# Batch 0's queries cut as 192 and 256 instead of 256 and 192, with other loads at the start, in a fused attention and FFN kernel

## The chip, the core and the metric

The kernel runs on one core of a Trainium2 chip. Its time is the device time of one execution in microseconds; the median of several runs counts. A profile is one further execution, recorded by the hardware profiler. PE is TensorE, ACT is ScalarE, DVE is VectorE, POOL is GpSimd, SP is SyncE. Times within a profile are microseconds from the start of the span.

## The reference

Eight batches of attention with twelve heads, 448 tokens and head size 64, with a sigmoid in the place of the softmax, then a gated feed-forward network (FFN) over all 3584 tokens.

```python
scores = (1 / sqrt(64)) * q @ k.transpose(0, 1, 3, 2) - log(448)
attn = 1 / (1 + exp(-scores))
x = (attn @ v)                     # heads joined: 3584 x 768
gate = maximum(x @ w_gate, 0)      # 768 x 1536
val = x @ w_val                    # 768 x 1536
out = (gate * val) @ w_out         # 1536 x 768
```

Inputs and output are fp32 in memory; the kernel computes in fp16 with sums in fp32.

## The kernel before

**Tiles.** A batch's q, k and v lie in SBUF as fp16, 128 partitions by head pairs and token chunks. Twelve heads make three groups (g) of four heads, 448 tokens make seven chunks (c) of 64. `pe_transposes` (L201, copied out by DVE at L206) or, from batch 2 on, `dma_transposes` turn a group's k and q into `qkT`. `qk` (L232) computes scores for one chunk of keys in four 64x64 corners of the PE array, ACT takes the sigmoid into `PT` (L187), `pv` (L250) multiplies with v, and DVE scales the result into `xT` (L184). `gv` (L309) is one FFN unit: 128 of the 1536 hidden columns (f from 0 to 11), six matmuls for the gate and six for the value, then a relu (DVE at L320 or ACT at L318) and a product on DVE (L327) into `hT`.

**Order.** The program order is written by hand; each engine works through its own queue in that order. DMA issues stand in the queue of their engine as well: SP and ACT issue through hardware queues, POOL through a software queue, which also turns fp32 into fp16 on the way. POOL holds at most eight software loads in flight, since each waits for the semaphore of the eighth before it.

**Batch 0.** It is the stage that the change touches. Its queries are cut in two at `QCUT` = 4 chunks: `HALVES` are 256 queries and then 192. A `FirstSlot` is one group with one half: slots 0 to 2 are groups 0 to 2 with the first half, slots 3 to 5 the same with the second. A slot has four units `(i, u)`: three with two chunks of keys, one with a single chunk. A unit's scores go into one of two PSUM buffers (`pairp`), and one ACT instruction takes the sigmoid of all of it. The dictionary `after` says what PE does behind each unit: transposes of the next group, `keep_warm` (matmuls on zeros), `pv` of an earlier slot, or `ffn_mix(n)`, which takes n units from `gv_queue`. The queue is filled by `push_first(half, fs)`; a unit of half 0 needs the x of slots 0 to 2, one of half 1 that of slots 3 to 5. Four PSUM banks serve all the rest of this stage.

**Loads of batch 0.** The first four k chunks and the first `QCUT` q chunks of group 0 come in fp32 by SP and ACT into `ysb` tiles (L126) and are cast by DVE (L604) and ACT (L605). All else comes by POOL: the last three k chunks of group 0, k and the first q chunks of groups 1 and 2, the rest of group 0's q, v in three parts, then the FFN weights of two or three f at a time (`load_gv`, L148) between the loads of batch 1.

**Batch 1.** Its scores run in six bursts; behind each burst the tuple `mix` gives the count of `gv` units, and `hooks` place transposes among them: `(left, job)` runs the job when `left` units of that mix remain. From batch 2 on, the FFN uses sums of blocks to save products (L385); this part is not touched.

Of the kernel before, what the change touches and what calls it, by code (L numbers as in the profile page):

```python
# [17 lines left out]
def kernel(  # L18
# [10 lines left out]
    nc = tc.nc  # L29

    B, H, S, D = q.shape
# [4 lines left out]
    NCH = S // 64  # L36
    NDC = DM // P
    NFC = DF // P
    TW = 2 * NCH
    QCUT = 4  # L40
    HALVES = ((0, QCUT), (QCUT, NCH))

    qk_scale = 1.0 / math.sqrt(D)
# [59 lines left out]
    def rows_of(src, b):  # L103
        return src[b].rearrange("(x r) (t c) d -> (r t) x (c d)", r=2, c=NCH)

    def load(b, g0, g1, which, c0=0, c1=NCH):
        for nm, t16, src in zip("kq", tiles_of(b), (k, q)):
            if nm in which:
                xs, cs = slice(2 * g0, 2 * g1), slice(c0 * D, c1 * D)
                nc.gpsimd.dma_start(t16[:, xs, cs], rows_of(src, b)[:, xs, cs])  # L110

    def load_v(b):
        v16 = tiles_of(b)[2]
        nc.gpsimd.dma_start(v16[:, 0::2, :], rows_of(v, b)[:, 0::2, :])
        for r in range(2):
            nc.gpsimd.dma_start(
                v16[64 - 64 * r : P - 64 * r, 1::2, :], rows_of(v, b)[64 * r : 64 * r + 64, 1::2, :]
            )


    KCUT = 4
    first32 = []
    for src, c1, eng in ((k, KCUT, nc.sync), (q, QCUT, nc.scalar)):
        ysb = ysbp.tile([P, DM], FP32, tag="ysb", name="ysb")
        t32 = ysb[:, 0 : 2 * c1 * D].rearrange("p (x y) -> p x y", x=2)
        eng.dma_start(t32, rows_of(src, 0)[:, 0:2, 0 : c1 * D])  # L126
        first32.append(t32)
    zeros = early.tile([P, S], FP16, name="zeros")
    nc.vector.memset(zeros[:], 0.0)  # L129
    ident = early.tile([P, P], FP16, name="ident")  # L130
    make_identity(nc, ident[:])
    load(0, 0, 1, "k", KCUT)
    gate = const.tile([P, 2], FP16, name="gate")
    for g in range(1, NG):
        load(0, g, g + 1, "k")
        load(0, g, g + 1, "q", 0, QCUT)
    load(0, 0, 1, "q", QCUT)
    load_v(0)

    wg = wpool.tile([P, NDC, DF], FP16, name="wg")  # L140
    wv = wpool.tile([P, NDC, DF], FP16, name="wv")
# [2 lines left out]
    def load_gv(f0, f1, which=(0, 1)):  # L144
        fs = slice(f0 * P, f1 * P)
        for i in which:
            wt, src = ((wg, moe_w_gate), (wv, moe_w_val))[i]
            nc.gpsimd.dma_start(wt[:, :, fs], src[:, fs].rearrange("(c p) f -> p c f", p=P))  # L148
# [2 lines left out]
    load(0, 1, NG, "q", QCUT)  # L151
    load_gv(0, 2, (1,))
    load_gv(2, 4)
    load_gv(4, 6)
    load(1, 0, 1, "kq")
    load_gv(6, 9)
    load(1, 1, 2, "kq")
    load_v(1)
    load_gv(9, 12)
    load(1, 2, 3, "kq")  # L160

    def load_o():
        for m0, m1 in ((0, 512), (512, DM)):
# [31 lines left out]
    def pe_transposes(b, g, ti, c0=0, c1=NCH):  # L195
        t16 = in_tiles[b][ti]
        qkT = qkT_of(b, g)
        trt = bank16("trt")
        for c in range(c0, c1):
            for h in range(2):  # L200
                nc.tensor.transpose(  # L201
                    trt[64 * h : 64 * h + 64, c * P : (c + 1) * P],
                    t16[:, 2 * g + h, c * D : (c + 1) * D],
                    ident[:],
                )
        nc.vector.tensor_copy(  # L206
            qkT[:, ti * NCH + c0 : ti * NCH + c1, :].rearrange("p c x -> p (c x)"),
            trt[:, c0 * P : c1 * P],
        )
# [378 lines left out]
    def push_first(half, fs, act_relu=True):  # L588
        c0, c1 = HALVES[half]
        push_gv(0, 64 * c0, 64 * (c1 - c0), fs, act_relu)  # L590
# [12 lines left out]
    k16, q16, _ = in_tiles[0]  # L603
    nc.vector.tensor_copy(k16[:, 0:2, 0 : KCUT * D], first32[0])  # L604
    nc.scalar.copy(q16[:, 0:2, 0 : QCUT * D], first32[1])  # L605
    pe_transposes(0, 0, 0, 0, KCUT)
    pe_transposes(0, 0, 1, 0, QCUT)
    keep_warm(2)
    slots = [FirstSlot(half * NG + g, g, half) for half in range(2) for g in range(NG)]
    push_first(0, range(0, 6), False)  # L610
    def second_queries():
        for g in range(1, NG):
            pe_transposes(0, g, 1, QCUT, NCH)

    def pv_then_ffn(i):
        slots[i].pv()
        ffn_mix(1)

    def ffn_then_pv(i):
        ffn_mix(1)  # L620
        slots[i].pv()


    after = {
        (0, 0): lambda: pe_transposes(0, 0, 0, KCUT, NCH),
# [5 lines left out]
        (1, 2): lambda: pe_transposes(0, 2, 1, 0, QCUT),  # L631
        (1, 3): lambda: keep_warm(2),
        (2, 0): lambda: keep_warm(2),
        (2, 1): lambda: pe_transposes(0, 0, 1, QCUT, NCH),
        (2, 2): slots[0].pv,
        (2, 3): slots[1].pv,
        (3, 1): slots[2].pv,
        (3, 2): second_queries,
        (3, 3): lambda: ffn_mix(1),
        (4, 1): lambda: ffn_then_pv(3),  # L640
        (4, 3): lambda: ffn_mix(2),
        (5, 1): lambda: pv_then_ffn(4),
        (5, 3): lambda: ffn_mix(1),
    }
    for i, slot in enumerate(slots):
# [2 lines left out]
            if (i, u) in after:  # L648
                after[(i, u)]()
    slots[5].pv()  # L650
    push_first(1, range(0, 6))
    for f0 in range(6, 12, 2):
        for half in range(2):
            push_first(half, range(f0, f0 + 2))

# [59 lines left out]
    for b in range(1, B):  # L715
        if b == 1:
            cuts, pv_at = (0, 3, 6, 9, 13, 17, 21), {3: (0, 2), 5: (1, 2)}
        else:
            cuts, pv_at = (0, 4, 7, 11, 14, 18, 21), {0: (-1, 2), 2: (0, 2), 4: (1, 2)}
        bursts = list(range(len(cuts) - 1))  # L720
        inner = None
        if b > 2:
            inner = 4 * (b % 2)
            bursts.remove(inner + 1)
        count = len(bursts)
        hooks = {}
        if b == 1:
            mix = (3, 3, 3, 3, 3, 2)
            hooks = {
                1: [(1, lambda: both(1, 1))],  # L730
                3: [(1, lambda: both(1, 2))],
                4: [(3, lambda: dma_transposes(2, 0))],
                5: [(2, lambda: dma_transposes(2, 1)), (0, late_loads)],
            }
        elif b == 2:
            mix = (2, 2, 1, 1, 1, 2)
            hooks = {
                2: [(0, prepare)],
                4: [(0, lambda: weight_sums(0))],
                5: [(1, lambda: weight_sums(1)), (0, lambda: weight_sums(2))],  # L740
            }
            open_late()
        elif b == 3:
            mix = (1, 1, 1, 0, 0)
        else:
            mix = (0,) * count

        def burst(n):
            for i, (g, c) in enumerate(order[cuts[n] : cuts[n + 1]]):
                if n in pv_at and i == pv_at[n][1]:  # L750
                    if n == 0:
                        pv_finish(b - 1)
                        if b == 2:
                            push_group(0)
                        elif b % 2 == 0:
                            push_group(b // 2 - 1)
                    else:
                        pv_group(b, pv_at[n][0])
                qk_unit(b, g, c)

        for m in range(count):
            jobs = []
            burst(bursts[m])
            if m == 0 and b > 2:
                jobs.append(lambda: dma_transposes(b, 2))
            if b == 2 and m == count - 1:
                jobs.append(lambda: (dma_transposes(3, 0), dma_transposes(3, 1)))
            elif b == 3 and m == count - 1:
                jobs.append(lambda: (dma_transposes(4, 0), dma_transposes(4, 1)))
            elif 0 <= m - count + 2 and 3 < b < B - 1:  # L770
                jobs.append(lambda: dma_transposes(b + 1, m - count + 2))
            if b == 1:
                if m == 0:
                    load(2, 0, 1, "kq")
                    load(2, 1, 2, "kq")
                    load(2, 2, 3, "kq")
                    load_v(2)
            elif m == 0 and b + 1 < B:
                if b == 3:
                    jobs.append(lambda: hold(3, 2))  # L780
                jobs.append(lambda: (load(b + 1, 0, 3, "kq"), load_v(b + 1)))
            if b % 2 and b > 2:
                if m == count - 1:
                    jobs.append(lambda: (batch_sums_t1(b // 2), batch_sums(b // 2, (0, 1))))
            elif b > 3 and m == 0:
                jobs.append(lambda: batch_sums(b // 2 - 1, (1, HD)))
            if b == 2 and m == count - 1:
                ffn_mix(mix[m], hooks[m])
                next_work(jobs + [lambda: weight_sums(3)], first_act=True)
            elif mix[m]:  # L790
                for job in jobs:
                    job()
                ffn_mix(mix[m], hooks.get(m, ()))
            else:
                next_work(jobs, amid=(lambda: burst(inner + 1)) if m == inner else None)
            if b == 3 and m in (1, 3):
                for f in range(*((0, 8, 2), (8, NFC, 2))[m // 2]):
                    gate_sums(f, f + 2)
# [35 lines left out]
```

## Time and profile before

| | |
|---|---|
| runs, median (lowest to highest) | 393.48 us (393.33 to 394.0), 3 runs |
| profiled execution | 393.23 us, span 391.5 us |
| granted PE clock | 1.00 |
| PE busy | 385.4 us, 98% of the span |
| ACT busy, DVE busy | 224.8 us, 278.7 us |
| first sigmoid of batch 0 | 6.95 us |
| first `gv` unit | 19.22 us |
| `pv` of slot 5 | 30.42 to 31.12 us |
| first scores of batch 2 | 62.01 us |

The timeline gives each engine's instructions with the time at which a run of equal ones starts, its length and the idle time ahead of it. The chain in order of time follows the work that ended last back from the end. Matmul times overlap, since they are pipelined: the distance from one start to the next is what an instruction holds PE.

Landings of some loads of before, by the DMA issues of narrow windows (issue time plus time to landing): first k on SP 4.1, first q on ACT 4.4, k tail of group 0 6.75, k of group 1 7.95, last part of v 14.34, wg of f = 0 and 1 16.35, wv of the same 19.32, the last load of batch 1 49.3.

### The profile page before, as it was taken

What the parts mean: (1) busy time and instruction counts of PE and PEld (TensorE: products, weight loads), DVE (VectorE), ACT (ScalarE), POOL (GpSimd) and SP (SyncE); (2) the same over time, 40 slices, a digit from 0 to 9 for tenths busy, and PEclk for the clock granted to TensorE, in tenths of its full rate; (3) what the DMA queues carried; (4) which work ended last, traced back from release to release, by engine and by line L of the source; (5) the groups of instructions that cost most, each with busy time, mean ns of one, the idle gap of its engine ahead of it and who ended that gap; (6) DMA issues with size and microseconds to landing.
All of it is one profiled execution on the core that took longest, in us unless ns stands there. A gap on an engine that the chain in (4) does not pass through costs nothing.

```text
span 391.5 us, 8755 instructions
## 1 busy us (share of the span) xinstructions
PE 385.4 (98%) x3494; PEld 215.3 (55%) x3494; DVE 278.7 (71%) x540; ACT 224.8 (57%) x476; POOL 49.5 (13%) x73
## 2 busy tenths in 40 slices
PE   8999999999999999999999999999999999999995
PEld 4678786445455545454555554545455555555553
DVE  2453444367378789999757789999767779987663
ACT  5946778784877755555547764545475434533122
POOL 8644310500030300003000300000000000000000
PEclk9999999999999999999999999999999999999999
DMA  9999999998799891226945694233013320000135
GB/s 153 198 200 205 204 200 138 155 202 144 176 166 201 161 218 27 47 49 78 174 97 130 126 228 67 39 43 62 3 41 82 82 80 2 0 3 0 40 88 156
DMA packets 68953, 43.69 MB, mean 112 GB/s; under 512 B 35888, under 2 KB 65584, under 8 KB 68912
## 3 DMA queue, kind: packets, MB, share of 16 engines
q0 software_dynamic: 30736, 23.33, 39.7%
q1 hardware_dynamic: 37664, 19.24, 23.9%
q10 hardware_dynamic: 512, 0.56, 0.5%
q8 instruction: 27, 0.44, 0.4%
q14 instruction: 14, 0.11, 0.1%
HBM read 47.19 MB, written 11.01 MB: 149 GB/s over the span
## 4 chain that ended last, share of the span: by engine, by line
PE 96%; ACT 2%; DVE 1%; issue 0%
PE u L385 33%; PE g L385 16%; PE qk_ps L232 9%; PE y L385 9%; PE pv_ps L250 8%; PE g_ps L309 8%; PE v_ps L309 7%; PE ya L346 3%; ACT PT L187 2%; PE yb L346 1%; PE trt L201 1%; PE warm_ps L175 1%; DVE qkT L206 0%; DVE ysb L483 0%; DVE zeros L129 0%
## 5 line engine op out<-in xcount | busy, mean ns | idle before, releaser
L187 ACT ACTIVATE PT<-qk_ps 128x448 f16<-128x448 f32 (+3 forms) x318 | 150.8, 587 | 77.8 <-PE qk_ps L232 77.7
L385 PEld LDWEIGHTS <-S 128*128 128x128 f16 x540 | 52.8, 98 | 43.6 <-issue 0.2
L554 DVE TENSOR_TENSOR gsb<-g,gsb 128x448 f32<-128x448 f32 x72 | 42.8, 624 | 13.6 <-PE g L385 13.3
L232 PE MATMUL qk_ps<-qkT 64*64 64x448 f16 (+2 forms) x756 | 47.3, 335 | 0.9 <-DVE qkT L206 0.5
L327 DVE TENSOR_TENSOR hT<-gate_sb,v_ps 128x256 f16<-128x256 f32 (+2 forms) x36 | 16.2, 465 | 34.0 <-ACT gate_sb L318 18.0
L550 ACT COPY gsb<-u 128x448 f32<-128x448 f32 x48 | 25.6, 558 | 24.0 <-PE u L385 22.9
L385 PEld LDWEIGHTS <-hT 128*128 128x128 f16 x294 | 27.5, 98 | 21.3 <-issue 4.7
L421 ACT ACTIVATE ysb<-u 128x384 f32<-128x384 f32 x28 | 13.7, 490 | 42.7 <-PE u L385 40.6
L184 DVE TENSOR_SCALAR xT<-pv_ps 128x448 f16<-128x448 f32 (+2 forms) x53 | 27.9, 567 | 13.3 <-PE pv_ps L250 12.0
L250 PE MATMUL pv_ps<-PT,v 64*64 64x448 f16 (+2 forms) x756 | 36.5, 329 | 0.0
L309 PE MATMUL g_ps<-xT,wg 128*128 128x256 f16 (+2 forms) x216 | 33.5, 291 | 0.1
L309 PE MATMUL v_ps<-xT,wv 128*128 128x256 f16 (+2 forms) x216 | 33.3, 290 | 0.0
L385 PEld LDWEIGHTS <-wg 128*128 128x128 f16 x216 | 20.1, 98 | 21.8 <-issue 4.3
L385 PEld LDWEIGHTS <-wv 128*128 128x128 f16 x216 | 21.1, 98 | 19.7
L232 PEld LDWEIGHTS <-qkT 64*64 64x64 f16 x756 | 17.8, 105 | 21.8 <-issue 13.5
L250 PEld LDWEIGHTS <-v 64*64 64x64 f16 x756 | 21.4, 107 | 11.1 <-issue 0.7
L439 DVE SCALAR_TENSOR_TENSOR ysb<-y,ysb 128x384 f32<-128x384 f32 x24 | 13.4, 557 | 18.2 <-PE y L385 10.4
L385 PE MATMUL u<-T,hT 128*128 128x384 f16 x138 | 26.2, 326 | 0.0
L309 PEld LDWEIGHTS <-wg 128*128 128x128 f16 x216 | 18.5, 98 | 11.7 <-issue 5.1
L110 POOL DMA_DIRECT2D k<-in_k_dram x14 | 10.9, 777 | 109.1 <-DVE rel L215 102.7
L309 PEld LDWEIGHTS <-wv 128*128 128x128 f16 x216 | 20.2, 98 | 7.4
L385 PE MATMUL u<-xT,wg 128*128 128x448 f16 x108 | 23.5, 354 | 0.0
(69 smaller groups left out, 532.2 us busy)
## 6 DMA issues: line engine op xcount, KB each, us to landing
out_dram<-ysb SPq DMA_DIRECT2D x52, 192.0 KB, 3.0
k<-in_k_dram POOLq DMA_DIRECT2D x5, 672.0 KB, 11.7
q<-in_q_dram POOLq DMA_DIRECT2D x5, 672.0 KB, 14.5
v<-in_v_dram POOLq DMA_DIRECT2D x8, 336.0 KB, 14.7
v<-in_v_dram POOLq DMA_DIRECT2D x16, 168.0 KB, 14.0
k<-in_k_dram POOLq DMA_DIRECT2D x8, 224.0 KB, 12.0
wo<-in_moe_w_out_dram POOLq DMA_DIRECT2D x1, 1536.0 KB, 11.2
q<-in_q_dram POOLq DMA_DIRECT2D x6, 224.0 KB, 12.3
```

The lines of the kernel that those rows point to most:

```text
L184: nc.vector.tensor_scalar(out=xT, in0=src, scalar1=XSCALE, scalar2=None, op0=AOP.mult)
L187: nc.scalar.activation(PT_ap, ps_ap, AF.Sigmoid, bias=sig_bias, scale=qk_scale)
L232: nc.tensor.matmul(out_of(hh)[o : o + 64, :], qkT[rows, c, cols], qkT[rows, NCH + c0 : NCH + c1, cols], start=True, stop=True, tile_positi ...
L250: nc.tensor.matmul(ps[hh][64 * r : 64 * r + 64, 0:qn], v16[rows, 2 * g + hh, c * D : (c + 1) * D], pieces[c][rows, hh, :], start=(c == 0), ...
L309: nc.tensor.matmul(ps[-1][:, 0:qn], wt[:, dc, f * P : (f + 1) * P], xT_tiles[b][:, dc, q0 : q0 + qn], start=(dc == 0), stop=(dc == NDC - 1),)
L327: nc.vector.tensor_tensor(out=hT_tiles[g][:, f, o : o + qn], in0=gate_sb[:, 0:qn], in1=ps[1][:, 0:qn], op=AOP.mult,)
L346: nc.tensor.matmul(ps[:, 0 : m1 - m0], hT_tiles[g][:, f, t * P : (t + 1) * P], wo[:, f, m0:m1], start=(f == 0), stop=(f == NFC - 1),)
L385: nc.tensor.matmul(ps[:, 0:n], A[:, k_, :], W[:, k_, :], start=(first and k_ == 0), stop=(k_ == kn - 1), skip_group_check=True,)
L421: nc.scalar.activation(o, ps[:, 0:HM], AF.Copy, scale=OUT_SCALE)
L439: nc.vector.scalar_tensor_tensor(out=o, in0=ps[:, 0:HM], scalar=OUT_SCALE, in1=o, op0=AOP.mult, op1=AOP.add)
L550: by(gs[u][i][:], ps[u][:, 0:S])
L554: nc.vector.tensor_tensor(out=gs[u][i][:], in0=ps[u][:, 0:S], in1=gs[u][i][:], op=AOP.add)
```

## The change

The first part of batch 0's queries becomes 192, the second 256. The last three k chunks of group 0 come in fp32 by SP, behind the first k load, and ACT casts them, ahead of the first sigmoid. POOL loads v before the rest of group 0's queries. Among the later loads, batch 1's k and q come between weights at other places, and the last `load_gv` is parted. The rest of group 0's q is transposed behind unit (2, 3) instead of (2, 1), where a `keep_warm` stands now; `pv` of slot 2 and the second queries' transposes come one unit earlier. In slots 3 to 5 four `gv` units of 192 columns run instead of six of 256; batch 1 has 19 units in its mixes instead of 17.

```diff
-    QCUT = 4
+    QCUT = 3
...
-    for src, c1, eng in ((k, KCUT, nc.sync), (q, QCUT, nc.scalar)):
+    for src, c0, c1, eng in (
+        (k, 0, KCUT, nc.sync), (q, 0, QCUT, nc.scalar), (k, KCUT, NCH, nc.sync)
+    ):
         ysb = ysbp.tile([P, DM], FP32, tag="ysb", name="ysb")
-        t32 = ysb[:, 0 : 2 * c1 * D].rearrange("p (x y) -> p x y", x=2)
-        eng.dma_start(t32, rows_of(src, 0)[:, 0:2, 0 : c1 * D])
+        t32 = ysb[:, 0 : 2 * (c1 - c0) * D].rearrange("p (x y) -> p x y", x=2)
+        eng.dma_start(t32, rows_of(src, 0)[:, 0:2, c0 * D : c1 * D])
...
-    load(0, 0, 1, "k", KCUT)
     gate = const.tile([P, 2], FP16, name="gate")
     for g in range(1, NG):
         load(0, g, g + 1, "k")
         load(0, g, g + 1, "q", 0, QCUT)
+    load_v(0)
     load(0, 0, 1, "q", QCUT)
-    load_v(0)
...
     load_gv(2, 4)
+    load(1, 0, 1, "kq")
     load_gv(4, 6)
-    load(1, 0, 1, "kq")
+    load(1, 1, 2, "kq")
     load_gv(6, 9)
-    load(1, 1, 2, "kq")
     load_v(1)
-    load_gv(9, 12)
+    load_gv(9, 12, (0,))
     load(1, 2, 3, "kq")
+    load_gv(9, 12, (1,))
...
     nc.scalar.copy(q16[:, 0:2, 0 : QCUT * D], first32[1])
+    nc.scalar.copy(k16[:, 0:2, KCUT * D : NCH * D], first32[2])
...
-    push_first(0, range(0, 6), False)
+    push_first(0, range(0, 4), False)
...
+    def first_queries():
+        pe_transposes(0, 0, 1, QCUT, NCH)
+        slots[1].pv()
...
-        (2, 1): lambda: pe_transposes(0, 0, 1, QCUT, NCH),
+        (2, 1): lambda: keep_warm(2),
         (2, 2): slots[0].pv,
-        (2, 3): slots[1].pv,
-        (3, 1): slots[2].pv,
-        (3, 2): second_queries,
+        (2, 3): first_queries,
+        (3, 0): slots[2].pv,
+        (3, 1): second_queries,
         (3, 3): lambda: ffn_mix(1),
-        (4, 1): lambda: ffn_then_pv(3),
-        (4, 3): lambda: ffn_mix(2),
-        (5, 1): lambda: pv_then_ffn(4),
+        (4, 1): lambda: pv_then_ffn(3),
+        (4, 3): lambda: ffn_mix(1),
+        (5, 1): slots[4].pv,
         (5, 3): lambda: ffn_mix(1),
...
-    push_first(1, range(0, 6))
-    for f0 in range(6, 12, 2):
+    push_first(1, range(0, 4))
+    for f0 in range(4, 12, 2):
...
-            mix = (3, 3, 3, 3, 3, 2)
+            mix = (3, 3, 3, 4, 4, 2)
```

## The prediction

> **What bounds the kernel now.** I began with the page's busy shares and its chain that ended last.
>
> ```profile
> PE 385.4 (98%) x3494; PEld 215.3 (55%) x3494; DVE 278.7 (71%) x540; ACT 224.8 (57%) x476; POOL 49.5 (13%) x73
> PE 96%; ACT 2%; DVE 1%; issue 0%
> ```
>
> TensorE sets the end, except for 2% of ScalarE. The busy times by stretch say where PE ever idles.
>
> ```profile
> 5.00:17.34 12.34, 11.45 (x232) 6.98 (x231) 4.57 (x11) 10.08 (x13) 10.03 (x14) 1.00 1.35 191
> 17.34:31.12 13.78, 13.78 (x273) 10.97 (x273) 8.12 (x22) 8.01 (x12) 5.96 (x9) 1.00 1.40 200
> ```
>
> Columns: stretch, length, busy time of PE, PEld, DVE, ACT and POOL, granted clock, DMA share, GB/s. PE idles 0.89 us before 17.34 and not at all in the 13.78 us after it; the later stretches show 0.06 us up to 62.01 and none from there to the last matmul at 387.5. So every microsecond of PE time lost or won in the first stage reaches the end of the program. The chain in order of time shows what holds PE before 17.34:
>
> ```profile
> 10.11 0.44 PE qk_ps L232 x8
> 10.55 0.02 issue
> 10.58 3.35 ACT PT L187 x4
> 13.92 0.02 issue
> 13.94 3.35 ACT PT L187 x4
> 17.30 0.04 issue
> 17.34 0.36 PE qk_ps L232 x8
> ```
>
> A slot here is one group of four heads times one part of the queries: four units of scores, then their sigmoids. Slots 1 and 2 (256 queries) are bound by ScalarE, 3.36 and 3.40 us from start to start. PE fills that time with score matmuls, transposes and keep_warm, because no FFN work exists until x is complete for three groups. The timeline of ScalarE shows the other regime:
>
> ```profile
> 17.34 2.60 ACT L187 ACTIVATE PT<-qk_ps 128x768 f16<-128x768 f32 x4
> 21.11 1.51 ACT L187 ACTIVATE PT<-qk_ps 128x768 f16<-128x768 f32 x2 [1.16 <-PE qk_ps L232]
> 23.55 1.19 ACT L187 ACTIVATE PT<-qk_ps 128x768 f16<-128x768 f32 x2 [0.94 <-PE qk_ps L232]
> 26.65 1.51 ACT L187 ACTIVATE PT<-qk_ps 128x768 f16<-128x768 f32 x2 [1.91 <-PE qk_ps L232]
> 29.10 1.19 ACT L187 ACTIVATE PT<-qk_ps 128x768 f16<-128x768 f32 x2 [0.94 <-PE qk_ps L232]
> ```
>
> A slot of 192 queries costs ScalarE 2.62 us, and in slots 4 and 5 it idles 4.95 us, waiting for PE, which is busy with six FFN units. The timeline of PE prices these:
>
> ```profile
> 19.22 0.83 PE L309 MATMUL g_ps<-xT,wg 128*128 128x256 f16 x6
> 19.89 0.82 PE L309 MATMUL v_ps<-xT,wv 128*128 128x256 f16 x6
> 20.64 0.52 PE L232 MATMUL qk_ps<-qkT 64*64 64x192 f16 x16
> ...
> 30.42 0.77 PE L250 MATMUL pv_ps<-PT,v 64*64 64x192 f16 x28
> 31.12 0.58 PE L201 MATMUL trt<-ident,k 128*64 128x128 f16 x14
> ```
>
> One gv unit of 256 columns holds PE from 19.22 to 20.64, 1.42 us (1.32 where another follows, 23.46 to 24.78); one of 192, 32.02 to 33.12, 1.10 us (1.00, 33.81 to 34.81). The attention of batch 0 is through at 31.12, with six gv units of 256 done.
>
> **The cut of the queries, first half.** The narrow part comes first, so slots 0 to 2 need 2.62 us of ScalarE each. I walk PE's order with the rows' durations. The first sigmoid starts at 6.83 (6.95 before): the copy of six q transposes takes 0.35, not 0.43. Slot 0's sigmoids end at 9.49. Slot 1 needs group 1's k transposes, which stand after the third unit (whose score buffer is freed at 7.64, but keep_warm holds PE to 7.82): transposes from 8.12, k copy 0.63 us to 9.30, q copy 0.35 to 9.66, scores at 9.71, sigmoid at 10.12. ScalarE idles 0.63 there, where the longer slot left 0.28. Slot 2 starts at 13.04 in the same way and its sigmoids end at 15.78 (17.30 before). Slot 3 needs the rest of group 0's queries: these transposes now stand behind pv(0) and the scores at 14.93, run from 15.14, and their copy waits on DVE behind the two xT operations of pv(0); pv(1) holds PE from 15.55 to 16.15; the scores run then and slot 3's first sigmoid is at 16.61 (17.34 before). So 1.5 us of shorter sigmoids become a lead of 0.73, and ScalarE has idled 0.83 us once more.
>
> **Second half.** Slots 3 to 5 now have 256 queries: 3 x 3.38 = 10.1 us of sigmoids in place of 7.9. Beside them PE has only four gv units of 192, 4 x 1.10 = 4.4 us, where it had 6 x 1.42 = 8.5. PE's own work from 16.15 to the last pv is then about 10.2 us (scores 2.6 at 0.21 a full unit, as from 15.02 to 15.23, and 0.13 where another kind follows, pv(2) 0.6, 16 transposes 0.8, gv 4.4, pv(3) and pv(4) 1.6, changes between kinds 0.2). ScalarE and PE are nearly equal and wait for each other in turn: ScalarE idles 0.27 behind the first gv and 0.48 behind pv(3) and the second gv, PE 0.25, 0.27, 0.70 and 0.08 for score buffers and the last sigmoid. The last sigmoid ends at 27.7 and pv(5) (0.76 us) at 28.5.
>
> **Sum.** At 28.5 the changed kernel has four gv of 192 done, before had six of 256 at 31.12. The difference, 6 x 1.32 - 4 x 1.00 = 3.9 us, is still to be done, in the bursts of batch 1 (mix 19 in place of 17). So 28.5 + 3.9 = 32.4 against 31.12. The same walk through the order of before gives 31.24 where the trace has 31.12, so I take 0.1 off: +1.2 us. By PE's account: idle 1.9 in place of 0.9, one keep_warm pair more at (2,1) 0.48 (10.46 to 10.94), two gv units fewer that stand alone -0.2: +1.3. With PE gapless afterwards, 1.2 us arrive at the end.
>
> **Loads.** The tail of k goes by SP's queue behind the first k load, in fp32, and ScalarE casts it. Queued behind that cast are all sigmoids. No row shows a second load on SP: issued near 1.2 behind the first, it lands near 4.6 if as quick (3.4 us), near 6.5 if as slow as the software tail was (5.3 us). On SP nothing else is queued until 54 us. I take 5.1, since these two loads land at 4.1 and 4.4 and 192 KB more at the 304 GB/s of 2.00 to 3.50 is 0.65 us. With a cast of about 0.5 us, less than the 0.62 of 128x512, that is 5.6, hidden before 6.83; at the slow end the first sigmoid starts 0.3 late, and the total by as much. The gain is nil: the tail of before landed at 6.75 and held nobody for more than 0.2 us.
>
> Without the tail, with narrower q parts and q's rest behind v, POOL issues v some 1.5 us earlier (5.85 before; 0.73 an issue) and the software queue reaches it sooner (last v landed 14.34, I expect 12.3 to 13.3; pv(0) wants it at 14.3), and q's rest at 13.0 to 14.0, wanted at 15.14. Then wg and wv of the first two f: wv landed at 19.32, I expect 18.3 to 19.3; the first gv now wants it at 19.3 (19.89 before). Its cover is thin: a late wv delays PE by as much, at most 0.3 if nothing arrives sooner and the hardware tail slows the queue by 0.3.
>
> ```profile
> 2.00:3.50 1.50, 1.50 (x6) 0.61 (x5) 0.00 (x0) 0.76 (x2) 1.50 (x3) 1.00 0.95 304
> 3.50:5.00 1.50, 1.50 (x5) 0.33 (x3) 0.57 (x1) 0.57 (x1) 1.50 (x3) 1.00 0.95 100
> 6.50:8.00 1.50, 1.50 (x24) 0.64 (x24) 0.36 (x1) 1.05 (x2) 1.38 (x3) 1.00 1.31 193
> ```
>
> The last two columns say that from 3.50 to 5.00, while the hardware loads run out and the software queue begins with the small tail, only 100 GB/s move: the tail in fp32 fits there. [...]
>
> Weights of f = 2 to 5, batch 1's k, q and v trade places in the queue; each is wanted later than before (f = 4 first at about 36 us, not 27), so nothing is priced. The move of load(1,2) before the last wv leaves that wv at most at 49.3, where the last load of the group landed; f = 9 wants it near 51.
>
> **Batch 2's transposes.** In the fifth burst of batch 1 the mix of 4 puts dma_transposes(2, 0) behind one gv: its copies come some 2 us later (issue 54.23, now near 56.2). That transpose landed 7.7 us after issue, at 61.93, and the scores of batch 2 began at 62.01: no slack. They now begin at 63.2. Later ones, with fewer loads beside them, landed 5.2 and 5.7 after issue, so I expect 61.6 to 62.6 and price nothing; at 7.7 it is 63.9 and costs 0.7 us. On the side of a gain the same step caps it, since the transposes can't come much before 61.
>
> **The rivals.** ScalarE is fed without gaps (faster): 6.83 + 3 x 2.62 + 3 x 3.38 = 24.8 for the last sigmoid, pv(5) ends at 25.6, with 3.9 to follow 29.5: with the 0.1 taken off -1.7 us at the very best, 391.5. It decides once ScalarE's lost time in slots 0 to 5 falls from my 2.9 us below 1.7; against it stand the 0.63 and 0.83, which are chains of copies and transposes that the trace shows at these lengths, and the cap above. With lost time near 0.9 the median is 392.7. I give it 0.1. The two halves cancel: the lead of 0.73 grows to 1.3 at slot 3 because a copy or pv comes sooner, PE waits less, and the sum is 0 to 0.7: 393.5 to 394.2; 0.2. A load or the transpose of batch 2 joins the loss: 1.2 + 0.3 to 1.0, 395.0 to 395.7; 0.2. My forecast itself: 0.5.
>
> **How the numbers follow.** The profiled execution took 393.23 us (span 391.5 and 1.7 around it), the median is 393.48. 393.23 + 1.2 = 394.4 in a profile, 394.7 as a median. The range of 8 in 10 leaves out the gapless case and the upper tail: 393.6 to 395.9. What a measurement of this kernel can tell is about 0.2%, 0.8 us: faster 0.1, within it 0.2, slower 0.7.
>
> **What would show it.** Right: sigmoids of 128x768 first, from about 6.8, ScalarE idle near 9.5 and again near 16; first gv near 18.8; PE idle of some tenths between 24 and 28 released by ScalarE; pv(5) near 27.7; scores of batch 2 near 63.2. Wrong: pv(5) before 26.5, or no PE idle between 16 and 28, means the gapless rival; PE waiting for wv, or for the transpose at 63, means the third.

## The result and the profile after

| | before | after |
|---|---|---|
| median of 6 runs each, us | 393.51 (393.33 to 394.36) | 395.61 (395.4 to 396.77) |
| ratio, 95% interval | | 1.0054 (1.0043 to 1.0065) |
| profiled execution; its span, us | 393.23; 391.5 | 396.77; 395.0 |
| first sigmoid | 6.95 | 7.31 |
| `pv` of slot 5 starts; ends | 30.42; 31.12 | 29.81; 30.69 |
| first scores of batch 2 | 62.01 | 65.49 |

The change costs 2.1 us: slower, as forecast, and within the range, but 0.9 us more than forecast. The profiled execution of after lies 1.16 us above its median. Full PE clock began at 7.10 us in it, at 5.61 in the profile of before, and that moves the first sigmoid: the two `keep_warm` matmuls ahead of the first scores held PE 0.85 us in after (5.90 to 6.75), 0.65 in before (5.84 to 6.49). So stretches are compared below from the first sigmoid on. From batch 2's first scores to the last matmul both kernels take 325.4 to 325.5 us: the whole loss lies ahead of batch 2.

The page of after, its busy shares and its chain:

```profile
PE 387.0 (98%) x3496; PEld 215.3 (55%) x3496; DVE 277.0 (70%) x538; ACT 226.6 (57%) x479; POOL 48.7 (12%) x72
PE 97%; ACT 1%; issue 1%; DVE 0%; ACTq 0%
```

"issue" had 0% of the chain before and has 1% now: time in which an engine waits for nothing that the profile shows. The busy times of PE, PEld, DVE, ACT and POOL in stretches of after (then granted clock, DMA share, GB/s):

```profile
5.00:17.34 12.34, 11.60 (x242) 6.41 (x245) 4.07 (x11) 8.24 (x13) 9.39 (x14) 1.00 1.35 190
17.34:31.12 13.78, 11.89 (x267) 9.17 (x259) 6.32 (x19) 10.14 (x12) 5.84 (x8) 1.00 1.39 200
31.12:62.01 30.89, 30.83 (x420) 24.73 (x418) 12.02 (x30) 21.80 (x55) 8.54 (x12) 1.00 1.15 182
```

In the second stretch PE was gapless before and idles 1.89 us now. ScalarE's timeline has the two halves as predicted, 2.60 us of sigmoids a slot (four units), then 3.34:

```profile
7.31 2.60 ACT L189 ACTIVATE PT<-qk_ps 128x768 f16<-128x768 f32 x4 [2.18 <-PE qk_ps L234]
10.52 5.58 ACT L189 ACTIVATE PT<-qk_ps 128x768 f16<-128x768 f32 x8 [0.60 <-PE qk_ps L234]
17.42 3.34 ACT L189 ACTIVATE PT<-qk_ps 128x1024 f16<-128x1024 f32 x4 [1.32 <-PE qk_ps L234]
21.27 1.94 ACT L189 ACTIVATE PT<-qk_ps 128x1024 f16<-128x1024 f32 x2 [0.50 <-PE qk_ps L234]
24.89 4.94 ACT L189 ACTIVATE PT<-qk_ps 128x1024 f16<-128x1024 f32 x6 [1.69 <-PE qk_ps L234]
```

It idles 1.69 us ahead of 24.89, where I had 0.48 behind pv(3) and the second gv. PE's waits from 5 to 62 us of after (in total, times, longest) and its timeline say why:

```profile
PE pv_ps L252 <- issue: 1.2, 2, 0.9
PE qk_ps L234 <- ACT PT L189: 0.9, 2, 0.5
PE qk_ps L234 <- DVE qkT L208: 0.5, 1, 0.5
```

```profile
15.79 0.69 PE L252 MATMUL pv_ps<-PT,v 64*64 64x192 f16 x21
16.74 0.36 PE L252 MATMUL pv_ps<-PT,v 64*64 64x192 f16 x7 [0.25 <-issue]
...
21.20 0.81 PE L252 MATMUL pv_ps<-PT,v 64*64 64x256 f16 x21
22.93 0.41 PE L252 MATMUL pv_ps<-PT,v 64*64 64x256 f16 x7 [0.92 <-issue]
...
28.48 0.30 PE L234 MATMUL qk_ps<-qkT 64*64 64x256 f16 x4 [0.50 <-ACT PT L189]
```

The waits for ScalarE (0.40 at 19.41, 0.50 at 28.48) were in the prediction in kind. The two pauses inside pv(1) and pv(3) were not: 1.17 us in which no semaphore holds PE, in the middle of a run of equal matmuls whose inputs were all there (slot 3's last sigmoid had ended at 20.76). The chain in order of time runs through the longer of them:

```profile
21.37 0.65 PE pv_ps L252 x21
22.02 0.92 issue
22.93 0.41 PE pv_ps L252 x7
```

**A theory for the pauses.** They stand ahead of matmuls 224 and 352 of PE's program: 128 matmuls and 128 weight loads apart, 256 instructions. The page of after has a DMA queue of kind "instruction" with 27 packets of 16 KB; PE's 3496 matmuls and 3496 loads make 27.3 blocks of 256. (The count fits only roughly: the first of the 27 packets starts at 14.27, and from matmul 224 on there are 25.6 such blocks.) The answer for DMA traffic in a window shows one such packet in the stretch ahead of the second pause:

```profile
q0 software_dynamic: 480, 0.25, 139.2%
q8 instruction: 1, 0.02, 4.5%
```

That is 20.30 to 21.60 of after: the loads keep the engines full (139%), and the packet starts at 20.50 and takes 0.95 us. The trace has these packets at 14.27, 20.50 and 26.70 in after, and at 13.84, 20.04 and 26.24 in before: 6.2 us from one to the next in both, while the loads are queued. PE goes on 1.5 us after a packet's end (21.45 to 22.93, 15.22 to 16.74). So, by this theory, PE gets at most 256 instructions in 6.2 us here; where it reaches a block's end sooner, it stands. In before it reached the same two ends at 16.58 and 22.70, 0.2 to 0.3 us after the blocks were due (by the same sum at 16.3 and 22.5), and did not stop; the timeline of before has both `pv` in one piece:

```profile
16.11 0.96 PE L250 MATMUL pv_ps<-PT,v 64*64 64x256 f16 x28
22.50 0.77 PE L250 MATMUL pv_ps<-PT,v 64*64 64x192 f16 x28
```

The matmuls of `pv` are short: 28 of them hold PE 0.88 us (29.81 to 30.69), where the twelve of a gv unit of 192 hold it 1.09 (19.65 to 20.74). The change puts pv(3) ahead of the second gv (`pv_then_ffn`), and so the many short instructions ahead of the block's end.

### The profile page after: what moved, and what is told of

Read it like the earlier page. It is cut to its first block, busy times and chain, and to the rows that moved or that the text cites. A ratio compares the mean times of both kernels' runs of the same rounds, so it can differ in the third digit from the quotient of the medians.

```text
span 395.0 us, 8761 instructions
## 1 busy us (share of the span) xinstructions
PE 387.0 (98%) x3496; PEld 215.3 (55%) x3496; DVE 277.0 (70%) x538; ACT 226.6 (57%) x479; POOL 48.7 (12%) x72
## 4 chain that ended last, share of the span: by engine, by line
PE 97%; ACT 1%; issue 1%; DVE 0%; ACTq 0%
PE u L387 33%; PE g L387 16%; PE qk_ps L234 9%; PE y L387 9%; PE pv_ps L252 8%; PE g_ps L311 7%; PE v_ps L311 7%; PE ya L348 3%; PE warm_ps L177 2%; PE trt L203 1%; PE yb L348 1%; ACT PT L189 1%; DVE qkT L208 0%; DVE ysb L485 0%; DVE zeros L131 0%
## 5 line engine op out<-in xcount | busy, mean ns | idle before, releaser
L329 DVE TENSOR_TENSOR hT<-gate_sb,v_ps 128x192 f16<-128x192 f32 (+2 forms) x36 | 16.3, 465 | 35.6 <-ACT gate_sb L320 14.9
L552 ACT COPY gsb<-u 128x448 f32<-128x448 f32 x48 | 25.6, 558 | 24.0 <-PE u L387 22.9
L311 PE MATMUL g_ps<-xT,wg 128*128 128x192 f16 (+2 forms) x216 | 33.5, 291 | 0.1
L311 PE MATMUL v_ps<-xT,wv 128*128 128x192 f16 (+2 forms) x216 | 33.3, 290 | 0.0
L110 POOL DMA_DIRECT2D k<-in_k_dram x13 | 10.1, 779 | 108.5 <-DVE rel L217 102.7
```

The costliest lines, as they stand in the source:

```text
L311: nc.tensor.matmul(ps[-1][:, 0:qn], wt[:, dc, f * P : (f + 1) * P], xT_tiles[b][:, dc, q0 : q0 + qn], start=(dc == 0), stop=(dc == NDC - 1),)
L329: nc.vector.tensor_tensor(out=hT_tiles[g][:, f, o : o + qn], in0=gate_sb[:, 0:qn], in1=ps[1][:, 0:qn], op=AOP.mult,)
L552: by(gs[u][i][:], ps[u][:, 0:S])
```

## The experiments

Medians in us; "before" is the kernel before, run beside it. Its medians go from 393.67 to 393.99, so each kernel is compared with the one beside it. `early_loads`, `pv_first_before` and `earlier_q` are edits of before, all others of after.

| | median (runs) | before | ratio, 95% interval |
|---|---|---|---|
| `gv_first` | 394.95 (7) | 393.67 | 1.0033 (1.0022 to 1.0044) |
| `six_gv` | 395.29 (5) | 393.67 | 1.0038 (1.0025 to 1.0051) |
| `cut_only` | 395.91 (4) | 393.67 | 1.0058 (1.0043 to 1.0073) |
| `early_loads` | 393.53 (10) | 393.67 | 0.9994 (0.9985 to 1.0004) |
| `pv_first_before` | 394.44 (10) | 393.99 | 1.0013 (1.0003 to 1.0022) |
| `act_relief` | 395.06 (10) | 393.99 | 1.0031 (1.0021 to 1.0041) |
| `no_warm` | 394.86 (10) | 393.99 | 1.0028 (1.0017 to 1.0040) |
| `after_again` | 395.44 (5) | 393.86 | 1.0041 (1.0029 to 1.0054) |
| `five_gv` | 394.89 (8) | 393.86 | 1.0026 (1.0016 to 1.0036) |
| `earlier_q` | 393.62 (11) | 393.86 | 0.9990 (0.9981 to 0.9999) |
| `cut_best` | 394.73 (7) | 393.73 | 1.0026 (1.0015 to 1.0038) |
| `hold_loads` | 399.26 (1) | | |

**`gv_first`: the order at (4, 1) as before.**

```diff
-        (4, 1): lambda: pv_then_ffn(3),
+        (4, 1): lambda: ffn_then_pv(3),
```

> The changed kernel with one swap: behind unit (4, 1) the FFN unit comes before pv of slot 3, as it did in the kernel before. The profile of the changed kernel shows PE standing still for 0.92 us inside this pv (22.93) and 0.25 us inside pv of slot 1 (16.74), with no wait named, and just 256 PE instructions (weight loads and matmuls) lie between the two places. Theory F (PE's next block of 256 instructions has not been fetched yet): the swap puts 24 instructions that take 1.1 us ahead of pv matmuls that would take 0.33 us, so PE reaches the block's end about 0.77 us later: the standstill falls to 0.2 us or less, now before about the tenth matmul of pv, and the time falls by 0.6 to 0.8 us, to about 394.9. Theory D (pv of slot 3 waits for data: its sigmoids, v, or a PSUM bank): the wait stays inside pv or moves by the order alone, and the time stays at 395.4 to 395.8. Theory S of the prediction (ScalarE and PE wait for each other) says nothing about this pair, since the scores of (4, 2) come behind both in either order.

Its waits of PE have no "issue" any more:

```profile
PE qk_ps L234 <- ACT PT L189: 0.5, 1, 0.5
PE qk_ps L234 <- DVE qkT L208: 0.5, 1, 0.5
PE trt L203 <- DMA q<-in_q_dram: 0.2, 1, 0.2
```

394.95 us, 1.28 above before where after was 2.1 and, in `after_again`, 1.58 above. So the exchange of two pieces of work takes 0.3 to 0.8 us off; the intervals of `gv_first` and `after_again` overlap, and `pv_first_before` below tests the exchange by itself. In this profile both pauses are gone; the 0.50 for ScalarE is not. The pause at matmul 224 lies ahead of the exchange, which can't have removed it; it is nearly gone in `after_again` too.

**`six_gv`: the cut with six gv units in slots 3 to 5.**

```diff
-    push_first(0, range(0, 4), False)
+    push_first(0, range(0, 6), False)
...
-        (4, 1): lambda: pv_then_ffn(3),
-        (4, 3): lambda: ffn_mix(1),
-        (5, 1): slots[4].pv,
+        (4, 1): lambda: ffn_then_pv(3),
+        (4, 3): lambda: ffn_mix(2),
+        (5, 1): lambda: pv_then_ffn(4),
```

with the later loads and batch 1's mixes of before.

> The changed kernel with six FFN units of 192 in slots 3 to 5 at the places of the kernel before (FFN unit ahead of pv of slot 3, two behind (4, 3), one more behind pv of slot 4), with the mixes and the order of the later weight loads of before. Theory S (in slots 3 to 5 PE runs out of work beside ScalarE, idle 0.40 at 19.41 and 0.50 at 28.48): two more units go into idle time of PE; at most some 0.5 to 0.7 us are saved beyond the swap alone, 394.2 to 394.5, and the idle time near the end of slot 5 is gone. If ScalarE doesn't bind there: the units only move, and the time equals that of the swap alone, about 394.9. Theory F adds that the block's end inside pv of slot 3 is reached as in the swap alone.

The 0.50 us idle is gone, but the fifth unit waits for weights that land at 27.7:

```profile
27.72 0.67 PE L310 MATMUL v_ps<-xT,wv 128*128 128x192 f16 x6 [0.76 <-DMA wv<-in_moe_w_val_dram]
```

Six units of 192 columns are done sooner than six of 256 and run into the loads. The test is spoilt by this new wait; `five_gv` repeats it.

**`cut_only`: the cut with all loads as before.**

```diff
-    for src, c0, c1, eng in (
-        (k, 0, KCUT, nc.sync), (q, 0, QCUT, nc.scalar), (k, KCUT, NCH, nc.sync)
-    ):
+    for src, c0, c1, eng in ((k, 0, KCUT, nc.sync), (q, 0, QCUT, nc.scalar)):
...
+    load(0, 0, 1, "k", KCUT)
```

and so on for v, the rest of q and the later loads.

> The changed kernel with all loads as before: the tail of k by POOL, the rest of group 0's queries ahead of v, the later weight loads in the old order. Theories S and F: the loss is in the cut and the order of PE's work, so 395.2 to 395.8. Theory L (the loads cost it: the fp32 tail on the same engines, or weights that come in a worse order): 394.5 or less, and near 393.5 if it is all of it. Wanted times are met: last v lands near 14.2 for 14.7, wv of the first two f near 19.3 for 20.2.

395.91 us: no better than after. The pause at matmul 352 is here too (0.86 us at 22.41). The changed order of the loads is not the cause of the loss.

**`early_loads`: before with the early loads of the change.** The tail of k by SP, its cast on ACT, v ahead of the rest of q; the cut stays 256 and 192.

> The kernel before (256 first) with the early loads of the changed one alone: tail of k by SP in fp32 with the cast on ScalarE, v ahead of the rest of group 0's queries; the order of the later weights stays, since f = 4 is wanted at 27 us here. The prediction's price of nothing: 393.2 to 393.9. Theory L: 394 or more; a gain from the earlier v (it landed 1.4 us sooner in the changed kernel): 393.0 or less.

0.9994 (0.9985 to 1.0004): worth nothing and costing nothing. From 3.50 to 5.00, where before moved 100 GB/s, it moves 276 (last column):

```profile
3.50:5.00 1.50, 1.50 (x5) 0.33 (x3) 0.48 (x1) 0.42 (x1) 1.50 (x3) 1.00 1.10 276
```

**`pv_first_before`: before with the exchange alone.** `(4, 1): lambda: pv_then_ffn(3)`.

> The kernel before with one swap: behind unit (4, 1) pv of slot 3 comes before the FFN unit, the order of the changed kernel. Theory F (256 PE instructions per fetch, about 6.2 us from one block's start to the next one's arrival in this stage): in the kernel before the boundary fell on PE's matmul 352 at 22.78, with the block due near 22.45; with pv first PE gets there near 21.6, so it stands still for 0.7 to 0.9 us inside pv of slot 3, with no wait named, and the time is 394.2 to 394.6. If the standstill belongs to the cut and not to the order: no idle time, 393.4 to 393.9.

This is the theory's sharpest test, since before has no pause to begin with. PE's timeline:

```profile
21.24 0.67 PE L250 MATMUL pv_ps<-PT,v 64*64 64x192 f16 x23
22.64 0.32 PE L250 MATMUL pv_ps<-PT,v 64*64 64x192 f16 x5 [0.74 <-issue]
```

The pause appears at the same matmul 352, in another kernel with another cut, and the median rises by 0.45 us (in the profile the stage from the first sigmoid to batch 2 takes 0.98 more than in before).

**`hold_loads`: after, with the loads behind the first weights held back.** POOL waits for group 2's second queries before it issues them.

```diff
+    def held_loads():
+        nc.gpsimd.tensor_copy(gate[0:1, :], qkT_tiles[(0, 2)][0:1, TW - 1, 0:2])
+        load_gv(2, 4)
...
```

> The changed kernel, but POOL issues the loads from the weights of f = 2 on only after the second queries of group 2 are transposed (about 19.3 us), so that the software queue runs empty near 18 us. Theory F with the cause in the full DMA queues: the fetch that began at 20.5 (16 KB, queue of kind instruction) begins at 18 to 19, and the 0.92 us inside pv of slot 3 are gone or under 0.2; the one inside pv of slot 1 (0.25), ahead of the gap, stays. The late weights may cost PE up to 0.9 us at the third FFN unit, so the total (394.9 to 396) tells little. If the fetch takes its 6 us whatever the queues do, or the pause is a data wait: the 0.92 us stay.

The instruction packet that started at 20.50 in after, 6.2 us behind the one before it, starts at 18.30 here, 5.4 us behind the one before it; in the thirteen other profiles these are 6.0 to 6.2 us. Neither pause shows as an idle: matmul 352 starts 0.22 us after the one before it, where after has 1.18. That the pause at matmul 224 would stay was wrong. The weights come too late, which makes the time useless as a comparison:

```profile
PE v_ps L314 <- DMA wv<-in_moe_w_val_dram: 2.1, 1, 2.1
PE g_ps L314 <- DMA wg<-in_moe_w_gate_dram: 0.9, 1, 0.9
```

**`act_relief`: `gv_first` with less for ScalarE.** In slots 3 to 5 the fourth unit's sigmoid is left out; DVE writes the scaled scores in its place.

```diff
+            if self.number > 2 and u == 3:
+                nc.vector.tensor_scalar(
+                    out=PT[:, :, 0:n], in0=ps[:, :, 0:n], scalar1=qk_scale, scalar2=None, op0=AOP.mult
+                )
+            else:
+                sigmoid(PT[:, :, 0:n], ps[:, :, 0:n])
```

> gv_first with 0.6 us of ScalarE work less in each of slots 3 to 5: the fourth unit's sigmoid is left out, DVE writes the scaled scores instead. Theory S (in slots 3 to 5 the score buffers come free too late, since ScalarE has 10.1 us of sigmoids): the idle time of 0.50 us ahead of the scores of (5, 3), and the small ones of 0.08 and 0.06, go; 394.3 to 394.5. If PE's own work or a load sets the pace there: the time of gv_first, 394.9, within 0.2.

395.06 us, like `gv_first`, with 8.77 us of sigmoids in slots 3 to 5 where after has 10.22 (DVE has the rest of the work): my own reading that ScalarE's 10.1 us nearly equal PE's work and set the pace falls. PE's longest wait for ScalarE stays 0.5:

```profile
PE qk_ps L234 <- ACT PT L189: 0.9, 3, 0.5
```

That one is local: in slot 5 two sigmoids of 0.97 us must pass before a score buffer is free, and only pv(4) stands beside them.

**`no_warm`: `gv_first` without the new `keep_warm` at (2, 1).**

> gv_first without the pair of keep_warm at (2, 1). By PE's account of the prediction the pair costs 0.48 us: 394.45. By its walk along the chain less, since the scores of (2, 2) and (2, 3) wait for score buffers and pv of slot 0 for v (landed 12.94): 0.1 to 0.3 us, 394.7. If ScalarE alone sets the time up to 16 us: 0, 394.95.

394.86 us: 0.1 us less than `gv_first` by the medians, 0.4 by the distance to before beside each, not clearly the 0.48 that the matmuls hold PE. In the profile the stage takes 56.90 us, `gv_first` 56.79: PE idles 0.14 at 13.76, starts late at both ends of the theory's blocks (matmul 224 starts 0.37 us after the one before it, matmul 352 0.32) and waits 0.39 for ScalarE at 18.56:

```profile
PE qk_ps L234 <- ACT PT L189: 0.9, 2, 0.5
```

**`after_again`: after, unaltered.**

> The changed kernel unaltered, for a second profile beside the others. The first profile took 396.77 us, 1.2 above the median, with PE at full clock only from 7.10 us and the first sigmoid at 7.31; other profiles had full clock from 4.8 to 6.6 and the first sigmoid at 6.5 to 7.2. If the start's clock makes the difference, a profile with full clock near 5 has the first sigmoid near 6.5 and about 396.0. Theory F: PE's two pauses without a wait are there again, matmuls 224 and 352, 0.1 to 0.3 and 0.8 to 0.9 us, and the median is 0.6 to 0.9 above gv_first. If the pauses are an accident of one execution: gone, and the median equals gv_first within 0.3.

```profile
PE trt L203 <- DMA q<-in_q_dram: 0.8, 1, 0.8
PE qk_ps L234 <- ACT PT L189: 0.5, 1, 0.5
PE qk_ps L234 <- DVE qkT L208: 0.5, 1, 0.5
PE v_ps L311 <- DMA wv<-in_moe_w_val_dram: 0.3, 1, 0.3
```

Here the full clock began at 4.06 and the first sigmoid at 6.36. PE came to the rest of q of groups 1 and 2 before it had landed (17.56) and to wv as well (19.55); having stood 1.1 us there, it paused only 0.14 at matmul 352, not the 0.8 to 0.9 expected, and didn't idle at matmul 224. Loads and pauses add up to 1.26 us in this profile and to 1.17 in the other one. Of these two executions the earlier met the loads and the later one the two pauses; that this is a rule isn't shown (`five_gv`, with its first sigmoid at 6.38, waited for no load). By the theory both are waits for what the DMA queues have brought by then.

**`five_gv`: `gv_first` with one gv unit more, in slot 5, and the later loads in the order of before.**

```diff
-        (5, 1): slots[4].pv,
+        (5, 1): lambda: pv_then_ffn(4),
...
-            mix = (3, 3, 3, 4, 4, 2)
+            mix = (3, 3, 3, 4, 3, 2)
```

> gv_first with one more FFN unit of 192 in slots 3 to 5: one behind pv of slot 4 at (5, 1), one at (5, 3), and the old order of the later weight loads, so that wv of f = 4 lands near 27.4, about when the fifth unit wants it. In gv_first PE idles 0.50 us ahead of the scores of (5, 3), and leaving out sigmoids of slots 3 to 5 (act_relief) did not take this away: two sigmoids of slot 5 (1.93 us) must end for the buffer, and only pv of slot 4 stands beside them. Theory P (PE lacks an instruction there, at this place): the unit fills it, the idle time goes and 0.4 to 0.6 us with it, 394.3 to 394.6. If the idle time only moves to pv of slot 5 or to a wait for wv: 394.9.

```profile
PE qk_ps L233 <- DVE qkT L207: 0.5, 1, 0.5
PE qk_ps L233 <- ACT PT L188: 0.4, 1, 0.4
```

The 0.50 at slot 5 is gone, no idle with "issue" and no wait for a load is left in this view, and the kernel is still 1.0 us slower than before. The view doesn't show all, though: by the matmul records PE still starts matmul 352 0.30 us after the one before it and matmul 224 0.10 us, where the matmuls around them come every 0.00 to 0.10 us. A record's modelled end lies some 0.25 us after its start (by the means of before up to 62 us, 0.23 to 0.28 us for the shapes of up to 256 columns), so it covers the first 0.25 us of any wait.

**`earlier_q`: before, with the early loads, and the second queries transposed two units sooner.** q's rest of groups 1 and 2 is loaded ahead of wg, `second_queries` stands at (3, 0), and one `keep_warm` is out.

> A version that may beat both: the kernel before (256 first) with the early loads of the changed one, the rest of the queries of groups 1 and 2 loaded ahead of wg, their 12 transposes moved from (3, 2) to (3, 0), and without keep_warm at (2, 0). PE is gapless after 17.34 in the kernel before, and until then it has spare time; 12 transposes cost 0.45 us of PE. If they fit into the time that ScalarE sets up to 17.34: 0.3 to 0.45 us less than before, 393.1 to 393.3 on a median of 393.5. If they push the scores of (3, 1) back instead, or a fetch of instructions now ends inside pv of slot 3: no gain, 393.5 or more.

393.62 against 393.86, 0.9990 (0.9981 to 0.9999): at the edge of what can be told from no change; the 0.3 to 0.45 us that it was to gain didn't come. From first sigmoid to batch 2 it takes 55.00 us, before 55.06.

**`cut_best`: the best of the cut.** `five_gv` with q's rest of groups 1 and 2 ahead of wg, without `keep_warm` at (1, 3) and (2, 1).

> The kernel of five gv units (the 192-first cut, feed-forward units ahead of pv(3)), with the rest of q of groups 1 and 2 loaded ahead of the first weights, as it is wanted first, and without keep_warm at (1, 3) and (2, 1). Fetch theory (what is left of the loss is PE's place of work around two score buffers, the waits of some tenths for loads, and clock pads): no pause without a releaser, no PE wait for the rest of q; the removed keep_warm pairs bring at most 0.2 us together, because PE only waits at the same place for ScalarE: 394.4 to 394.6 us beside 393.7 to 393.9 for the kernel before. Rival one (the cut itself is harmless and only its schedule cost time): 393.5 to 393.8, no difference from before. Rival two (the weights, now behind more queries, make PE wait): a PE wait for wv of 0.3 us or more near 19, 394.9 or above.

394.73 us, 1.0026 (1.0015 to 1.0038). The forecast of 394.4 to 394.6 is missed by a little: where a `keep_warm` pair is gone PE waits 0.42 for ScalarE, at 12.48, and matmul 224 starts late again (0.33 us after the one before it). With everything mended that the waits of the profiles named, the cut of 192 and 256 is 1.0 us slower than that of 256 and 192. No version of it beat the kernel before.

## Why the prediction was right, and where it was wrong

What PE does from the first sigmoid to batch 2's first scores, in us: the distance from one matmul's start to the next, by kind, from the matmul records of each trace, with idles over 50 ns apart.

| | before | after | `gv_first` | `five_gv` |
|---|---|---|---|---|
| idle | 0.82 | 2.69 | 1.44 | 0.95 |
| scores | 10.58 | 11.08 | 11.19 | 11.30 |
| `pv` | 6.92 | 7.55 | 7.08 | 7.37 |
| gv units | 29.04 | 28.98 | 29.21 | 29.28 |
| transposes | 5.63 | 5.46 | 5.46 | 5.59 |
| `keep_warm` | 2.07 | 2.41 | 2.41 | 2.42 |
| sum | 55.06 | 58.17 | 56.79 | 56.91 |

**Right: the direction and its place.** The shorter first sigmoids gave little: from the first sigmoid to the scores of slot 3 the walk has 9.32 us (6.83 to 16.15), before 9.92, `gv_first` 9.18, after 9.54 with a pause of 0.25 inside. ScalarE idled 0.60 between slots 0 and 1, predicted 0.63. From the end of pv(5) to batch 2 after needs 34.80 us and before 30.89: 3.91 more, predicted 3.9. The tail of k landed at 4.60 (predicted 5.1), its cast ended at 5.14, and it held nobody. Batch 2's transpose landed at 64.34, later than my 61.6 to 62.6, but PE was later as well and waited for nothing at 65.49. That it held nobody was partly luck: it was issued at 60.30, not near 56.2, since its copies on DVE stand behind a product (59.18) that waits for ScalarE's relu, and that stands behind eight sigmoids; but it landed 4.0 us after issue, not 5.2 to 7.7.

**Right: the size of the forecast's own mechanism.** `gv_first`, the change without the pauses, is 1.28 us above before; the forecast was 1.2. (Its profile has 0.25 us of waiting for q, which the forecast hadn't.) Its pv(5) ends 21.99 us after the first sigmoid, by the walk 21.67 (6.83 to 28.5), in after 23.38.

**Wrong: a term that the sum hadn't.** The PE account had 1.9 us idle in place of 0.9. After idles 2.69 where before has 0.82, and of these 1.17 are the two pauses that the theory puts down to instructions; from matmul start to matmul start they are 0.49 and 1.18 us, of which 0.50 stand in the row `pv`. The sum had no term for the exchange in `pv_then_ffn(3)`. By medians it is 0.45 us in before (`pv_first_before`) and 0.3 to 0.8 in after. By the theory its cover was PE's program arriving in time, and no view that I showed of before has it: a chain with "issue 0%" doesn't say how near the next block was. The matmul records of the profiles show it (us; "behind its packet" is from the packet's end to the start of matmul 352, "behind matmul 351" from start to start):

| | before | `pv_first_before` | after | `after_again` | `cut_only` | `gv_first` | `no_warm` | `five_gv` | `cut_best` | `hold_loads` |
|---|---|---|---|---|---|---|---|---|---|---|
| behind its packet | 1.72 | 1.49 | 1.49 | 1.53 | 1.61 | 1.56 | 1.64 | 1.48 | 1.64 | 1.60 |
| behind matmul 351 | 0.00 | 0.98 | 1.18 | 0.42 | 1.12 | 0.00 | 0.32 | 0.30 | 0.06 | 0.22 |

In none of the 14 profiles does matmul 352 start sooner than 1.48 us behind its packet, or matmul 224 sooner than 1.29; where PE is late behind matmul 351 by more than 0.1 us, it is 1.48 to 1.64 behind the packet.

**Wrong in parts: the terms beside it.** Waits for ScalarE in slots 3 to 5 sum to 0.98 (0.40, 0.08 and 0.50), not to the 1.30 of the four that I listed; scores held PE 0.5 us longer than before, which my account hadn't: the first 0.25 us of a wait count to the matmul ahead of it, not as an idle, which can account for it. What the pair of `keep_warm` costs lies between 0.1 and 0.4 by the medians, and its 0.48 didn't come off in the profile. The 0.2 that two lone gv units fewer were to save isn't in the table (28.98 against 29.04). These misses nearly cancel, so the fit of `gv_first` is partly luck.

**Loads.** That the early loads bring nothing was right (`early_loads`, 0.9994), though from 3.50 to 5.00 us 276 GB/s moved in place of 100. wv landed at 18.95 in after, within the 18.3 to 19.3 expected, and at 19.55 in `after_again`, where it cost 0.30 us. The thin cover of wv was named with a price of at most 0.3 and left out of the sum; the rest of q of groups 1 and 2, which the second queries' transposes need, had no term at all. In `after_again` the two cost 0.30 and 0.82 us of idle. The rival "a load or transpose joins" had the right place on the number line (395.0 to 395.7) and half of the right cause.

**The other rivals.** Gapless ScalarE is out: it lost 4.1 us in its idles of 0.60, 1.32, 0.50 and 1.69, against the 1.7 from which that rival decides. That the halves cancel is out too: the lead did not grow to 1.3.

**Open.** How often unprofiled runs meet the pauses, the loads, or both can't be seen. Why `five_gv` and `cut_best` gain so little from the idle that they remove is settled in part: in `five_gv` 0.49 us less idle than in `gv_first` stands beside 0.29 more in `pv`, which is PE's late starts at matmuls 352 and 224 (0.30 and 0.10), and beside 0.13 more in transposes and 0.11 in scores, with runs that are too close to part by their medians. Without these late starts (0.40 us, in `cut_best` 0.39) the stage would take an estimated 56.5 and 56.3 us, before 55.06: what the cut itself loses there isn't taken apart further.

## What to carry to other kernels

Before making the first part of a job bound by ScalarE shorter, look whether the work beside it can follow; here it moved ScalarE's time into the part in which TensorE had work of its own to do, and that work was then done later. Where loads fill the DMA queues, count TensorE's instructions and look at the queue of kind "instruction": a pause put down to "issue" in the midst of a run of equal matmuls (0.25 and 0.92 us in after), a fixed number of instructions from the last one, was here, by the theory above, the program arriving late, and long matmuls ahead of the short ones at that place took the longer pause away (`gv_first`). Edits that only exchange two pieces of work weren't free on that count (0.45 us in `pv_first_before`). Look for such pauses in the distances from matmul start to matmul start: short ones don't show as idle here (0.30 us at matmul 352 in `five_gv`).

## What the runs showed of the hardware that was not expected

**Program code by DMA.** The traces of before and after each show 27 packets of kind "instruction", of 16 KB each, moving during the execution. Up to 33 us of the span, while software loads fill the engines, one starts 6.1 to 6.2 us behind the one before it (13.84 to 32.30 in before, 14.27 to 32.78 in after). PE paused 0.25 and 0.92 us in after, 0.74 in `pv_first_before` and 0.86 in `cut_only`, and went on 1.5 to 1.6 us behind the end of such a packet. That a packet is 256 of PE's instructions is inferred from the spacing of the pauses and the count; that PE waits there for the packet is inferred from these times and from `pv_first_before`; that the packets share the DMA engines with the loads is supported by `hold_loads`, where one came 5.4 us behind the one before it (one execution).

**The clock.** In `hold_loads` the granted clock fell to half at 25.28 us, as the windows show, and was full again from 32.10 on:

```profile
22.50:25.28 2.78, 0.91 (x18) 0.44 (x6) 0.54 (x2) 1.51 (x2) 2.78 (x5) 1.00 1.39 191
25.28:32.10 6.82, 5.74 (x72) 4.68 (x73) 1.47 (x4) 3.45 (x4) 3.28 (x5) 0.50 1.38 199
32.10:40.00 7.90, 7.90 (x118) 6.33 (x117) 3.34 (x8) 3.89 (x10) 3.12 (x4) 1.00 1.30 204
```

PE had idled 0.86 us (to 23.60) and then 1.0 us (from 24.27), with 0.67 us of work between them, when the clock fell. That the idles brought it down isn't shown: it is one execution, and no run varied them. The start of full clock moved between 4.06 and 7.10 us from profile to profile, two profiles of the same kernel among them, and with it the first sigmoid between 6.36 and 7.31. Ahead of that start the matmuls on zeros of 448 columns hold PE 0.37 us each in before and after (1.50 to 4.49), behind it 0.20 where another of them follows.
